# Two tiles transposed by DMA in place of TensorE, and two KV accumulations moved forward, in a linear-attention and SwiGLU kernel

## The chip, the core and the metric

The kernel runs on one core of a Trainium2 chip. A core has five engines, each with its own in-order instruction stream: TensorE (PE, matrix products; its weight loads are listed as PEld), VectorE (DVE), ScalarE (ACT), GpSimd (POOL) and SyncE (SP), which here issues nearly all DMAs. Engines wait for one another through semaphores. Operands live in SBUF (128 partitions); TensorE writes to PSUM, eight banks of 128x512 fp32.

The metric is the device time of one execution in microseconds, as a median of several executions. A smaller number is better.

## What is computed

The input x has 2048 rows (tokens) of 1024 values in bf16. Cut to what matters:

```python
xn = _layernorm(x)                                   # no affine part
q, k, v = split heads of (xn @ wqkv)                 # H = 32 heads of 32
phi = lambda t: where(t > 0, t + 1, exp(t)) + 1e-6
kv  = einsum("bhsd,bhse->bhde", phi(k), v);  z = sum over s of phi(k)
o   = (phi(q) @ kv) / (phi(q) . z + 1e-6)
s   = o @ wo
g   = silu((silu(xn @ w_gate) * (xn @ w_up)) @ w_down)   # F = 3584
return x + s * g
```

The KV matrix sums over all tokens, so all K and V products come before the first use of the attention's output.

## The kernel before

**Tiles.** x is cut into 16 tiles of 128 rows. For each tile, `x_load` brings it to SBUF, `ln_tile` normalises it and `t_tile` transposes it, so that the 1024 features lie on the partitions, as TensorE needs for a product over features. The transposed tiles of the first half of the tokens stay in the arena X, those of the second half in P.

**Normalising** (`ln_tile`, lines 767 to 795) is a chain of small operations: two statistics on VectorE (L772, L773), their aggregate (L778), an added epsilon (L779), a power on POOL (L782), and then, from tile two on, the negated mean on VectorE (L793) and the normalisation itself, one ScalarE activation of 128x1024 into W. The x tiles have four buffers, the normalised ones two: tile i uses buffer i mod 2, so tile four overwrites tile two's, and tile five tile three's.

**Transposing** (`t_tile`, lines 802 to 823) has two forms. Tiles below NPE (four before the change) are transposed by TensorE (L316): eight 128x128 transposes into one or more PSUM banks, and copies from there into X by ScalarE (L441) or VectorE (L823). Tiles two and three use one group of eight and one ScalarE copy of 128x1024 each. Tiles from NPE on are transposed by one DMA of SP (L808) from SBUF to SBUF, with no other engine.

**K and V products.** The first two tiles are multiplied plainly: eight calls of `p_piece`, each eight matmuls of 128x512. The other fourteen tiles go in seven pairs u = 1 to 7, and each pair has a K set (w = 0) and a V set (w = 1) (`kv_set`). A set multiplies two tiles by 1024 columns with seven products in place of eight (Winograd's form of Strassen's method). The products are numbered 1, 5, 2, 6, 7, 3, 4 in the order in which a set uses them; each is four matmuls of 128x512. Products 1, 2 and 4 take a transposed tile as it is: 1 and 2 the set's first tile, 4 its second. Products 5, 6, 7 and 3 take sums of the two tiles that VectorE makes (`x_sums`, four operations of 128x512 from X or P into W), so product 5 needs both tiles. The weights too need sums, made once on VectorE (`combos`).

A set's product 1 is copied to a second bank by ScalarE (`put1`), product 5 to SBUF (`put5`). VectorE adds product 5 in after products 6 and 7. A finished K block goes through `phi_evac` (an exponential on ScalarE, two operations on VectorE, L850 and L851), a V block through a ScalarE copy or, after product 7, a VectorE addition.

**KV accumulation.** `a_tile(i)` (lines 892 to 897) adds tile i's part to the KV matrix: eight matmuls of 128x129 into three banks that are kept for it. It needs all K and V blocks of tile i. The code puts these calls into a queue `fill` and takes one out in each set, after product 6 of the current set and product 1 of the next.

**What sets the order.** The code lists the operations in one program order, and `Plan` turns that into five instruction streams. It simulates the engines with costs written in the code. Each operation has a due time: the sum of TensorE's work listed ahead of its user, less the durations on the way. A DMA counts on that way as 4 us plus its bytes over 200 GB/s (line 112), and a transpose by DMA is entered with 400 KB, so it is due 6.05 us ahead of its user. VectorE, ScalarE, POOL and SP always take the ready operation that is due first. TensorE follows the program order, but may take an operation ahead of one that isn't ready, within a window of six (`WINDOW`). Then `tune` looks for gaps on TensorE and shifts due times where its simulation gets shorter. So any edit makes the whole order be planned again; on the chip the order of each engine is fixed.

The lines around the change, in the program order of the first tiles:

```python
ln_tile(2); p_piece(0, 1, 1); t_tile(2); combos(KVV[0], first[-1]); p_piece(1, 1, 1)
ln_tile(3); p_piece(0, 1, 0); t_tile(3); combos(KVV[1]);            p_piece(1, 1, 0)
```

After them come the first K set's products 1, 5 and 2 (L1001), and then the loop over the sets (L1003).

Of the kernel before, what the change touches and what calls it, by code (L numbers as in the profile page):

```python
# [316 lines left out]
    return last  # L317


def build_kernel(nc, A_x, A_wqkv, A_wo, B_w_gate, B_w_up, B_w_down, out, WINDOW=6, NWARM=15, NPE=4, LEAD=12.0):  # L320
    S, D, FF = 2048, 1024, 3584
    NT, KT, NG, NPAIR = 16, 8, 8, 14
    EPS_LN, EPS_PHI = 1e-5, 1e-6
# [9 lines left out]
    with ExitStack() as es:  # L333
# [20 lines left out]
        def named(*key):  # L354
            return Region([key])
# [50 lines left out]
        def bfree(b):  # L406
            freed[b] = len(PL.ops)
            (bare if b in is_bare else banks).append(b)
# [19 lines left out]
        def pe_mm(reads, writes, mms):  # L428
            return PL.op("pe", reads, writes, partial(_mm_group, mms), mm_cost(mms))
# [142 lines left out]
        for n in range(NWARM):  # L572
            b = n % 8
            m = 512 if n > 3 else 128
# [281 lines left out]
        def kv_ap(g):  # L856
            return ps[kvb[g // 3]][:, (g % 3) * 129:(g % 3) * 129 + 129]
# [34 lines left out]
        def a_tile(i):  # L892
            q = i % 4
            pk = pkv[i].ap()
            mms = [(kv_ap(g), pk[:, g * 128:(g + 1) * 128], vext[q][:, g, 0:129], i == 0 and g % 3 == 0, i == NT - 1)
                   for g in range(NG)]
            pe_mm([pkv[i].r, named("vx", q, 0), named("vx", q, 1), named("vx1", q), vx_r[q]], [bank_r[b] for b in kvb], mms)

        def x_sums(u):

            c = xs_ring.take()
            cv = c.ap(FP16).rearrange("p (m q t) -> p m q t", m=4, t=128)
            cr = [c.sub(q * KB, KB).r for q in range(4)]
            A = {(k, i): xt_half(2 * u + i, k) for k in range(2) for i in range(2)}
            ra = [xt_r(2 * u), xt_r(2 * u + 1)]
            tt(ra, [cr[0]], cv[:, 0], A[0, 1], A[1, 1], ALU.add, True)
            tt(ra + [cr[0]], [cr[1]], cv[:, 1], cv[:, 0], A[0, 0], ALU.subtract, True)
            tt(ra, [cr[2]], cv[:, 2], A[0, 0], A[0, 1], ALU.subtract, True)
            tt(ra + [cr[1]], [cr[3]], cv[:, 3], A[1, 0], cv[:, 1], ALU.subtract, True)

            def stat(m):
                if m in (1, 2, 4):
                    k, i = {1: (0, 0), 2: (1, 0), 4: (1, 1)}[m]
                    return [xt_ap(2 * u + i, 4 * k + q) for q in range(4)], ra[i]
                q4 = {5: 0, 6: 1, 7: 2, 3: 3}[m]
                return [cv[:, q4, q, :] for q in range(4)], cr[q4]
            return stat
# [56 lines left out]
        p_piece(1, 1, 0)  # L974
        for b in tb:
            bfree(b)
        fill = deque([partial(a_tile, 0), partial(a_tile, 1)])
        stats_of = {1: x_sums(1)}
        todo = [(u, w) for u in range(1, NT // 2) for w in range(2)]

        def prepare(u):
            if u >= NT // 2:
                return
            for i in (2 * u, 2 * u + 1):
                if i + 2 < NT:
                    x_load(i + 2)
            for i in (2 * u, 2 * u + 1):
                ln_tile(i)
                t_tile(i)
            stats_of[u] = x_sums(u)  # L990
# [3 lines left out]
        def kvs(n):  # L994
            if n not in sets and n < len(todo):
                u, w = todo[n]
                sets[n] = kv_set(u, w, stats_of[u])
            return sets.get(n)

        kvs(0)  # L1000
        for m in (1, 5, 2):  # L1001
            sets[0].step(m)
        for n in range(len(todo)):  # L1003
            cur = kvs(n)
            if todo[n][1] == 0:
                prepare(todo[n][0] + 1)
            nxt = kvs(n + 1)
            for m, k in ((6, 1), (7, 5), (3, 2), (4, 0)):
                cur.step(m)
                if nxt is not None and k:  # L1010
                    nxt.step(k)
                if k == 1 and fill:
                    fill.popleft()()
            if todo[n][1] == 1:
                while fill:
                    fill.popleft()()
                fill.extend((partial(a_tile, 2 * todo[n][0]), partial(a_tile, 2 * todo[n][0] + 1)))
# [730 lines left out]
def bass_recurrent_scan__linear_attn_block__swiglu_ffn__prompt_kernel(  # L1748
    nc: bass.Bass,
    A_x: bass.AP,  # L1750
    A_wqkv: bass.AP,
    A_wo: bass.AP,
    B_x: bass.AP,
    B_w_gate: bass.AP,
    B_w_up: bass.AP,
    B_w_down: bass.AP,
    out: bass.AP,
):
    build_kernel(nc, A_x, A_wqkv, A_wo, B_w_gate, B_w_up, B_w_down, out)
# [28 lines left out]
```

## Time and profile before

| | us |
|---|---|
| median of 5 runs | 716.21 (715.53 to 717.33) |
| profiled execution, its own time | 715.76 |
| span of its instructions | 714.0 |
| TensorE busy | 706.9 |
| VectorE busy | 641.7 |
| ScalarE busy | 404.5 |
| first transpose on TensorE (tile zero) starts | 6.54 |
| transposes of tiles two, three start | 18.11, 22.88 |
| first, second KV accumulation start | 24.19, 34.06 |
| first transpose by DMA (tile four) issued | 26.25 |

TensorE's granted clock is full in each slice of the span. All durations come from one profiled execution. In a timeline row the columns are start, length, engine and line, operation, what it writes and from what, how many instructions are merged in it, and in brackets the idle time of the engine before it and what ended that. Rows of one engine can overlap, because the matmuls are pipelined: the next starts before the one before has ended. The engine's name with a q is its instruction queue.

### The profile page before, as it was taken

To read this page: it belongs to the slowest core of one execution; us is meant where nothing else is said; L and a number is where in the kernel's file an instruction comes from. 1 tells how busy PE (TensorE), PEld (TensorE's weight loads), DVE (VectorE), ACT (ScalarE), POOL (GpSimd) and SP (SyncE) were. 2 spreads that over 40 slices of the span, in tenths; PEclk is the share of its full clock that TensorE was granted. 3 is DMA by queue.
4 is the path that set the end of the run, shared out by engine and by line. 5 is a ranking of instruction groups with operands and counts; after the bars stand their busy time and mean duration, and the time that the engine had idled before them with its cause. 6 is when DMAs were issued, how large, how long until landed. Compare 5 with 4: busy or idle time off the path is not lost.

```text
span 714.0 us, 11277 instructions
## 1 busy us (share of the span) xinstructions
PE 706.9 (99%) x4149; PEld 390.7 (55%) x4149; DVE 641.7 (90%) x1533; ACT 404.5 (57%) x779; POOL 12.5 (2%) x35
## 2 busy tenths in 40 slices
PE   8999999999999999999999999999999999999997
PEld 4444445555555555556556455555555555565654
DVE  7999988989999999998957999999999999798863
ACT  3666654887679675664122157676886656621212
POOL 2011000000000000000000000000000000000000
PEclk9999999999999999999999999999999999999999
DMA  9425335146364344225595964132715241656653
GB/s 306 107 60 118 60 117 177 60 125 215 135 186 130 126 137 134 86 84 164 149 197 164 257 169 148 60 118 92 202 66 177 89 148 60 175 143 161 143 155 95
DMA packets 138759, 98.11 MB, mean 137 GB/s; under 512 B 32849, under 2 KB 135761, under 8 KB 138705
## 3 DMA queue, kind: packets, MB, share of 16 engines
q1 hardware_dynamic: 138416, 97.21, 48.3%
q8 instruction: 32, 0.52, 0.3%
q10 hardware_dynamic: 288, 0.20, 0.1%
q14 instruction: 23, 0.18, 0.1%
HBM read 77.59 MB, written 12.71 MB: 126 GB/s over the span
## 4 chain that ended last, share of the span: by engine, by line
PE 91%; DVE 4%; DMA 2%; ACT 1%; issue 0%; SPq 0%; DVEq 0%
PE ps L309 91%; DMA X<-in_A_wqkv_dram 1%; DMA H<-in_A_wqkv_dram 1%; DVE TM L452 1%; DVE W L452 1%; DVE ps L452 1%; DVE X L452 1%; DVE H L851 1%; ACT TM L441 0%; ACT W L441 0%; DVE H L1035 0%; DVE P L452 0%; SPq L455 0%; ACT ps L441 0%; ACT L441 0%
## 5 line engine op out<-in xcount | busy, mean ns | idle before, releaser
L309 PE MATMUL ps<-X,W 128*128 128x512 f16 (+2 forms) x1372 | 289.2, 350 | 0.1
L441 ACT ACTIVATE TM<-ps 128x512 f16<-128x512 f32 (+3 forms) x355 | 186.7, 547 | 106.6 <-PE ps L309 102.8
L309 PE MATMUL ps<-H,W 128*128 128x512 f16 (+2 forms) x1096 | 218.9, 351 | 0.1
L452 DVE TENSOR_TENSOR W<-W 128x1024 f16<-128x1024 bf16 (+5 forms) x416 | 187.4, 487 | 6.2 <-PE ps L309 5.4
L309 PEld LDWEIGHTS ps<-X,W 128*128 128x128 f16 (+1 forms) x1372 | 132.7, 98 | 103.8 <-DVE ps L452 0.8
L309 PEld LDWEIGHTS ps<-H,W 128*128 128x128 f16 (+1 forms) x1096 | 106.2, 98 | 95.0 <-DVE ps L452 0.6
L452 DVE TENSOR_TENSOR ps<-ps,TM 128x256 f32<-128x256 f32 (+1 forms) x250 | 132.5, 532 | 12.6 <-PE ps L309 10.2
L441 ACT ACTIVATE ps<-ps 128x512 f32<-128x512 f32 (+1 forms) x174 | 85.4, 491 | 100.9 <-PE ps L309 100.5
L309 PE MATMUL ps<-P,W 128*128 128x256 f16 (+1 forms) x516 | 99.8, 319 | 0.4 <-DVE W L452 0.4
L441 ACT ACTIVATE H<-ps 128x512 f16<-128x512 f32 (+1 forms) x126 | 74.8, 604 | 41.4 <-PE ps L309 41.4
L452 DVE TENSOR_TENSOR H<-H 128x1024 f16<-128x1024 f16 (+5 forms) x126 | 71.9, 587 | 0.6 <-ACT H L441 0.4
L309 PEld LDWEIGHTS ps<-P,W 128*128 128x128 f16 (+1 forms) x516 | 50.3, 98 | 29.7 <-DVE W L452 0.7
L441 ACT ACTIVATE TM<-TM 128x512 f16<-128x512 f32 (+1 forms) x61 | 38.1, 626 | 48.8 <-DVE TM L452 48.8
L309 PE MATMUL ps<-W 128*128 128x256 f16 (+1 forms) x330 | 61.8, 282 | 0.2 <-DVE ps L452 0.2
L452 DVE TENSOR_TENSOR TM<-ps,TM 128x512 f32<-128x512 f32 (+3 forms) x63 | 41.8, 664 | 12.8 <-PE ps L309 12.1
L452 DVE TENSOR_TENSOR H<-H,TM 128x512 f16<-128x512 f16 x112 | 45.5, 420 | 8.4 <-ACT H L441 8.1
L309 PEld LDWEIGHTS ps<-W 128*128 128x128 f16 (+1 forms) x330 | 31.7, 98 | 32.2 <-DVE ps L452 2.3
L309 PE MATMUL ps<-H,X 128*128 128x512 bf16 (+1 forms) x150 | 35.6, 379 | 0.9 <-ACT ps L441 0.6
L309 PE MATMUL ps<-H,P 128*128 128x512 bf16 (+1 forms) x110 | 26.8, 379 | 0.0
L452 DVE TENSOR_TENSOR H<-ps,TM 128x512 f16<-128x512 f32 (+1 forms) x35 | 24.2, 690 | 2.6 <-PE ps L309 2.1
L452 DVE TENSOR_TENSOR TM<-TM,W 128x512 f16<-128x512 f16 (+1 forms) x39 | 14.4, 370 | 10.5 <-ACT TM L441 10.5
L309 PEld LDWEIGHTS ps<-H,X 128*128 128x128 f16 (+1 forms) x150 | 14.0, 98 | 17.1 <-ACT ps L441 1.1
(97 smaller groups left out, 433.8 us busy)
## 6 DMA issues: line engine op xcount, KB each, us to landing
W<-in_B_w_gate_dram SPq DMA_DIRECT2D x14, 1024.0 KB, 5.2
W<-in_B_w_up_dram SPq DMA_DIRECT2D x13, 1024.0 KB, 5.5
W<-in_B_w_down_dram SPq DMA_DIRECT2D x14, 896.0 KB, 6.1
H<-in_A_wqkv_dram SPq DMA_DIRECT2D x8, 512.0 KB, 8.0
H<-r_scratch SPq DMA_DIRECT2D x32, 128.0 KB, 3.5
W<-m_scratch SPq DMA_DIRECT2D x4, 1024.0 KB, 5.3
s_scratch<-TM SPq DMA_DIRECT2D x32, 128.0 KB, 2.3
TM<-in_A_x_dram SPq DMA_DIRECT2D x16, 256.0 KB, 3.4
```

The source lines that it names most:

```text
L309: last = h.matmul(o, l, r, start=st, stop=sp, skip_group_check=True)
L441: q = PL.op("act", reads, writes, lambda h: h.activation(o, i, func, **kw), nel(o) / (1000.0 if "bias" in kw or not isinstance(kw.get("sca ...
L452: return dve(reads, writes, lambda h: h.tensor_tensor(o, a, b, op), nel(o), 1.92 if fast else 0.96)
L851: dve([src_r, b.r], [out_r], lambda h: h.scalar_tensor_tensor(out_ap, src, 0.0, ba, ALU.max, ALU.add), 512)
```

## The change

The default of NPE goes from 4 to 2, so tiles two and three of x take the DMA form of `t_tile`. The queue `fill` starts empty; `a_tile(0)` is listed after product 1 of the first K set, and `a_tile(1)` after product 5, ahead of product 2. Later accumulations keep their places in the program order.

```diff
-def build_kernel(nc, A_x, A_wqkv, A_wo, B_w_gate, B_w_up, B_w_down, out, WINDOW=6, NWARM=15, NPE=4, LEAD=12.0):
+def build_kernel(nc, A_x, A_wqkv, A_wo, B_w_gate, B_w_up, B_w_down, out, WINDOW=6, NWARM=15, NPE=2, LEAD=12.0):
...
-        fill = deque([partial(a_tile, 0), partial(a_tile, 1)])
+        fill = deque()
...
         for m in (1, 5, 2):
             sets[0].step(m)
+            if m != 2:
+                a_tile(m // 5)
         for n in range(len(todo)):
```

## The prediction

> **What bounds the kernel now.** I read the page first, then the waits of TensorE, then the time around the change engine by engine: TensorE's timeline, the chain of work, VectorE's windows, the transposes by DMA. From the page:
>
> ```profile
> span 714.0 us, 11277 instructions
> PE 706.9 (99%) x4149; PEld 390.7 (55%) x4149; DVE 641.7 (90%) x1533; ACT 404.5 (57%) x779; POOL 12.5 (2%) x35
> ```
>
> TensorE (PE) is busy 706.9 of 714.0 us. So only two things shorten the run: work taken off TensorE, and idle time closed. All its named waits are few:
>
> ```profile
> PE ps L309 <- DVE TM L570: 1.0, 1, 1.0
> PE ps L316 <- DVE W L789: 0.8, 1, 0.8
> PE ps L309 <- ACT ps L441: 0.6, 1, 0.6
> PE ps L316 <- DVE TM L452: 0.6, 1, 0.6
> ```
>
> The first two lie before the first tile is transposed, the fourth at the end; the change touches only the third, 0.6 us. The timeline of TensorE shows where it lies:
>
> ```profile
> 18.11 0.61 PE L316 MATMUL ps<-ident,W 128*128 128x128 f16 x8
> 18.56 4.48 PE L309 MATMUL ps<-H,X 128*128 128x512 bf16 x20
> 22.88 0.61 PE L316 MATMUL ps<-ident,W 128*128 128x128 f16 x8
> 23.32 1.03 PE L309 MATMUL ps<-H,X 128*128 128x512 bf16 x4
> 24.19 0.63 PE L309 MATMUL ps<-H,TM 128*128 128x129 bf16 x8
> ...
> 28.87 1.04 PE L309 MATMUL ps<-H,X 128*128 128x512 bf16 x4 [0.59 <-ACT ps L441]
> ```
>
> The two rows on ident are the transposes of tiles two and three. 23.32 is product 1 of the first K set (tiles two and three), 24.19 the first KV accumulation (tile zero), 28.87 product 2 of the V set, which waits 0.59 us for ScalarE. The chain of work shows how ScalarE came to be late:
>
> ```profile
> 23.08 0.47 ACT H L441
> 23.55 0.03 issue
> 23.57 1.02 ACT X L441
> 24.59 0.49 ACT ps L441
> 25.08 2.27 ACT W L441 x2
> 27.35 0.97 ACT TM L441 x2
> 28.32 0.50 ACT ps L441
> 28.82 0.05 issue
> 28.87 21.21 PE ps L309 x115
> ```
>
> ScalarE runs without a break from 23.57 to 28.82, and the first step of that run is the 1.02 us copy of tile three out of PSUM.
>
> **The transposes on TensorE go.** Two groups of eight: the next row starts 18.56 - 18.11 = 0.45 and 23.32 - 22.88 = 0.44 us later. These starts, and not the 0.61 us durations, are the price, since matmuls are pipelined. Sum: **-0.89 us**, on the path, as TensorE has work on both sides. The Trainium skill (VectorE: DVE Perf Modes, "The three transpose paths") gives 390 ns for a 128x128 transpose on TensorE; by it sixteen would cost 6.2 us and the change would gain that much. The trace's pace is 56 ns, and I take the trace.
>
> **Their copies go too**, two of 1.02 us on ScalarE. The first (18.76) has nothing behind it that is late. The second heads the unbroken run above. Without it the last step ends at about 28.82 - 1.02 = 27.80. TensorE, which now runs dry at 28.28 (28.87 - 0.59), would get there at 28.28 - 0.89 + 0.47 = 27.86, the 0.47 being the second accumulation, which moves ahead of this place. So the wait closes: **between -0.59 and 0**. I take -0.5, since the products also change places among themselves and some of the wait may come back.
>
> **The accumulations move.** Each takes 24.66 - 24.19 = 0.47 us at the start-to-start pace; moving costs nothing by itself. What they read is there: the last K evacuation of tile one (L851) ends at 19.84, the V evacuations at 22.92 and 23.68, against earliest places of about 23.3 and 23.8. The second used to stand at 34.06, where VectorE is full; as filler it is missed there, which I count below.
>
> **What the DMA adds.** Two transposes on SP's queue:
>
> ```profile
> L808 SPq DMA_TRANSPOSE X<-W x4: 1237/1280/1342, 26.2 to 46.8; - x4
> DMA to landing us min/median/max: 3.0/3.1/3.5
> L1592 SPq DMA_TRANSPOSE TM<-TM x30: 1190/1214/3775, 355.3 to 705.1; - x30
> DMA to landing us min/median/max: 2.4/2.6/7.6
> ```
>
> Each holds SP's queue 1.24 us and lands a whole 128x1024 tile in 3.0 to 3.5 us here, up to 7.6 us later on, among the weight loads. The Trainium skill speaks against the change: its same table puts DMA at 1309 ns for a 128x128 block. Eight blocks in a row would be an estimated 10.5 us; tile three, ready at 22.43, would land at 32.9 and leave TensorE idle for some 7 us. Twelve rows at L808 of the same shape say 3.0 to 3.5 us, so I use these for the likeliest and the 7.6 for the range.
>
> *Tile two* leaves normalisation at 17.86 (ScalarE, 16.62 + 1.24). Its transpose is issued about 17.9, when the initial weight load still drains, and an x load issued at 17.88 took 4.7 us to land. So it lands between 20.9 and 22.6. Its first user, product 1 of the K set, moves to 23.32 - 0.89 = 22.43, and the accumulation of tile zero can fill a gap. Cost 0 to 0.2; I take 0.
>
> *Tile three* leaves normalisation at 22.43 if nothing is reordered, and lands at 25.5 to 26.0; the first operand sum on VectorE takes 0.42 us, so product 5 could start at 25.9 to 26.4. The cover: from 22.43 on TensorE has product 1 (0.86), both accumulations (0.94), product 2 (0.86) and product 1 of the V set (0.86), all of which do without tile three, and that the planner's window of six lets ahead: 3.52 us, to 25.95. Stall 0 to 0.45. But the planner counts a transpose by DMA as 6 us ahead of its user, so tile three's normalisation gets a due time some 4 us earlier. In the trace its x tile landed at 15.4, its statistics start at 17.10, and its small operations on VectorE and POOL end at 21.16 for work of about 2.8 us: 1.3 us can come out of that stretch alone, which brings the landing to about 24.3. I take a stall of 0. Without the two accumulations between, the cover is 2.58 us and the same landing at 25.5 would stall product 5 by about 0.9.
>
> *Who waits behind them.* SP issues in order: x tiles six and seven (17.88, 22.45) go out 1.2 us later, and tiles four and five's transposes (26.25) follow. Tile six's statistics are taken after 36.0, so 10 us of slack. Normalised tiles four and five reuse two and three's buffers and now wait for the DMA's read to land: 22.6 against 24.99, and 24.3 to 25.5 against 26.2. Cost 0; with tile three at 27 or later ScalarE would be held, and the next set with it. POOL does one power (0.55 us) per tile and idles otherwise.
>
> **What VectorE gives back.** Its windows:
>
> ```profile
> 18.00:28.00 10.00, 10.00 (x66) 5.16 (x64) 9.36 (x27) 8.50 (x12) 1.64 (x3) 1.00 0.31 90
> 28.00:40.00 12.00, 11.40 (x60) 5.34 (x59) 11.85 (x26) 5.99 (x11) 0.12 (x1) 1.00 0.34 80
> ```
>
> Columns: window, length, then busy PE, PE weight loads, VectorE, ScalarE, POOL. From 18 to 40 us VectorE is busy 21.2 of 22, and its work isn't reduced. TensorE 1.4 us early meets a VectorE that can be at most 0.8 us early. So up to 0.6 us may return as short waits between 28 and 45; after 50 VectorE has 4 us spare in 50 (45.90 busy). I take +0.2: LayerNorm of later tiles and operand sums can be put off.
>
> **Sum:** -0.89 - 0.5 + 0 + 0.2 = **-1.2 us**: span 714.0 to 712.8, the profiled execution 715.76 to 714.6. That execution is 0.45 us under the median of 716.21, so the median goes to **715.0** (-0.17%). A measurement of this kernel tells about 0.2% (1.43 us) from no change, so this sits just inside.
>
> **The rivals.**
> *VectorE takes it all back.* For it: 97% busy in 28 to 40. Against it: 0.8 us of idle time that it can use. The gain shrinks to 0.2 to -0.5 us of loss: 716.0 to 716.7.
> *More than the sum.* A replanned order also closes a little of the idle time later (TensorE's named waits from 50 us on sum to 1.2 us, half of it at the very end) and all 0.59 goes: -1.5 to -2.1 us, 714.1 to 714.7. For it: the order is recomputed whole. Against: nothing later is aimed at.
> *Slower: tile three lands late at product 5.* Place: 25.95 on TensorE. Each microsecond of landing after 25.5 costs one. Landing 4.7 us after issue (as the x load) at 22.45 stalls TensorE by 1.6 us and gives about 716.6; the 7.6 us row gives a landing at 30.0, a stall of 4.5 and 719.5. It decides (slower by 0.2%) from a landing at about 28.2, 5.7 us after the issue. Against: DMA share falls to near nothing after 20 us.
> *The work isn't moved at all:* excluded, sixteen transposes leave the program.
>
> **How the numbers follow.** Chances: forecast (714.3 to 715.8) 0.48; more than the sum 0.16; VectorE takes it back 0.18; late tile three or a worse replanned order 0.18. Faster by over 0.2% means under 714.78: the second case and 0.42 of the first, 0.36. Slower means over 717.64: the last case where it is beyond its point, 0.16. The rest is 0.48. The range reaches from 713.8 (leaving 0.05 below) to 717.8 (leaving 0.14 above); the likeliest case's own is 714.3 to 715.8.
>
> **What the changed profile would show.** L316 of TensorE with sixteen instructions fewer; the 128x1024 copies into X at L441 gone; L808 into X with six issues. TensorE's timeline after the last piece: product 1, two 128x129 groups within 3 us, then product 5 without a wait on VectorE's sums; no 0.59 us wait for ScalarE near 28. Wrong would be a wait of product 5 on the W sum (late tile three), short waits on VectorE between 28 and 45 that sum to over 0.6, or new idle time past 100 us, where no step of mine reaches.

## The result, and the profile after

The changed kernel takes 714.9 us (713.81 to 715.82) against 716.3 us (714.96 to 717.64) for the kernel before, measured anew beside it. The ratio is 0.9981, with a 95% interval of 0.9975 to 0.9987. So it is faster, by 1.4 us, which is 0.19%: clear of no change by its interval, and just inside the 0.2% that the prediction had set as its bound. Two later measurements of the same kernel gave 0.9984 (0.9975 to 0.9992) and 0.9985 (0.9976 to 0.9993), that is 1.1 to 1.2 us.

The page of the changed kernel, first lines:

```profile
span 713.2 us, 11248 instructions
PE 706.2 (99%) x4133; PEld 389.7 (55%) x4133; DVE 641.0 (90%) x1533; ACT 403.4 (57%) x777; POOL 13.2 (2%) x35
```

Sixteen matmuls and two ScalarE instructions are gone, VectorE has as many as before. The waits of TensorE:

```profile
PE ps L309 <- DVE TM L570: 1.0, 1, 1.0
PE ps L316 <- DVE W L789: 0.7, 1, 0.7
PE ps L309 <- DVE ps L452: 0.6, 1, 0.6
PE ps L316 <- DVE TM L452: 0.6, 1, 0.6
PE ps L309 <- DVE W L452: 0.4, 1, 0.4
```

The 0.6 us wait for ScalarE has left the list. A wait for VectorE's PSUM work has come (0.6 us, third row); it lies near 409 us, far from the change, and the last section shows that it differs between executions of the same order. TensorE's timeline around the change:

```profile
11.14 12.27 PE L309 MATMUL ps<-H,X 128*128 128x512 bf16 x56
23.25 1.10 PE L309 MATMUL ps<-H,TM 128*128 128x129 bf16 x16
24.19 1.89 PE L309 MATMUL ps<-H,X 128*128 128x512 bf16 x8
26.02 2.85 PE L309 MATMUL ps<-H,W 128*128 128x512 f16 x12
28.70 1.03 PE L309 MATMUL ps<-H,X 128*128 128x512 bf16 x4
29.56 2.75 PE L309 MATMUL ps<-H,W 128*128 128x512 f16 x12
32.15 1.03 PE L309 MATMUL ps<-H,X 128*128 128x512 f16 x4
33.17 1.90 PE L309 MATMUL ps<-H,W 128*128 128x512 f16 x8
```

No transposes stand in it. After the plain products and product 1 of the first K set (within the 56) come both accumulations (23.25, sixteen matmuls), then product 2 and the V set's product 1 (24.19), then product 5 (26.02). That is the order which the prediction gave. Idle time can be read from the starts: 512-wide matmuls start 0.216 us apart, so eight from 24.19 end their turn at 25.92, and the next starts at 26.02, 0.10 later. From 26.02 twelve lead to 28.61 against 28.70, 0.09; from 32.15 four lead to 33.01 against 33.17, 0.16. Together 0.35 us between 23 and 40 us. In the kernel before, the four from 27.25 led to 28.11 and the next started at 28.87: 0.76 us, which the profile named as 0.59. The sum for the stretch is then -0.89 for the transposes and -0.41 for idle time: -1.30 us. In the two later profiles of the changed kernel the idle time of the stretch is 0.23 and 0.27 us.

The two tiles' own DMAs, and VectorE's windows:

```profile
L808 SPq DMA_TRANSPOSE X<-W x6: 1237/1289/1522, 16.3 to 44.4; - x6
DMA to landing us min/median/max: 3.0/3.0/4.4
18.00:28.00 10.00, 10.00 (x59) 4.78 (x57) 9.86 (x26) 7.25 (x11) 2.59 (x3) 1.00 0.77 162
28.00:40.00 12.00, 12.00 (x56) 5.23 (x55) 11.74 (x26) 6.38 (x11) 0.55 (x1) 1.00 0.22 62
```

Tile two's transpose was issued at 16.26 and landed 4.4 us later, at 20.7, while the first weights still came in. Tile three's was issued at 20.89 and landed at 23.9. VectorE is busy 9.86 of 10 us from 18 to 28 (9.36 before): it used the idle time that it had.

### The profile page after: what moved, and what is told of

Its sections match the earlier page's. It is cut to its first block, busy times and chain, and to the rows that moved or that the text cites. A ratio compares the mean times of both kernels' runs of the same rounds, so it can differ in the third digit from the quotient of the medians.

```text
span 713.2 us, 11248 instructions
## 1 busy us (share of the span) xinstructions
PE 706.2 (99%) x4133; PEld 389.7 (55%) x4133; DVE 641.0 (90%) x1533; ACT 403.4 (57%) x777; POOL 13.2 (2%) x35
## 4 chain that ended last, share of the span: by engine, by line
PE 92%; DVE 4%; DMA 2%; ACT 1%; issue 0%; SPq 0%; DVEq 0%
PE ps L309 92%; DMA X<-in_A_wqkv_dram 1%; DMA H<-in_A_wqkv_dram 1%; DVE TM L452 1%; DVE W L452 1%; DVE ps L452 1%; DVE H L851 1%; DVE X L452 0%; ACT TM L441 0%; DVE H L1037 0%; DVE P L452 0%; SPq L455 0%; ACT L441 0%; DVE TM L850 0%; PE ps L316 0%
## 5 line engine op out<-in xcount | busy, mean ns | idle before, releaser
L309 PE MATMUL ps<-X,W 128*128 128x512 f16 (+2 forms) x1372 | 289.2, 350 | 0.1
L309 PE MATMUL ps<-H,W 128*128 128x512 f16 (+2 forms) x1096 | 218.5, 351 | 0.1
L309 PEld LDWEIGHTS ps<-X,W 128*128 128x128 f16 (+1 forms) x1372 | 132.7, 98 | 103.7 <-DVE ps L452 0.8
L309 PEld LDWEIGHTS ps<-H,W 128*128 128x128 f16 (+1 forms) x1096 | 105.9, 98 | 95.6 <-DVE ps L452 1.1
L309 PE MATMUL ps<-P,W 128*128 128x256 f16 (+1 forms) x516 | 99.8, 319 | 0.4 <-DVE W L452 0.4
L309 PEld LDWEIGHTS ps<-P,W 128*128 128x128 f16 (+1 forms) x516 | 50.3, 98 | 29.7 <-DVE W L452 0.7
L309 PE MATMUL ps<-W 128*128 128x256 f16 (+1 forms) x330 | 61.8, 282 | 0.7 <-DVE ps L452 0.6
L309 PEld LDWEIGHTS ps<-W 128*128 128x128 f16 (+1 forms) x330 | 31.7, 98 | 32.7 <-DVE ps L452 2.8
L309 PE MATMUL ps<-H,X 128*128 128x512 bf16 (+1 forms) x150 | 35.4, 379 | 0.3 <-DMA H<-in_A_wqkv_dram 0.2
L309 PE MATMUL ps<-H,P 128*128 128x512 bf16 (+1 forms) x110 | 26.8, 379 | 0.0
L309 PEld LDWEIGHTS ps<-H,X 128*128 128x128 f16 (+1 forms) x150 | 14.2, 98 | 17.3 <-DMA H<-in_A_wqkv_dram 0.9
```

Source lines behind the costliest of these rows:

```text
L309: last = h.matmul(o, l, r, start=st, stop=sp, skip_group_check=True)
```

## The experiments

The theory after the result: 0.9 us come from the transposes and the rest from the ScalarE wait, which the 1.02 us copy had caused. Rivals: the newly planned order brings the gain whatever was edited; or the accumulations do. A single profile's span is not used for differences below 1 us here, for a reason told at the end; times are medians, and idle time is read from starts inside a stretch.

**Parts put back with the order kept.** Three kernels keep every engine's planned order of the changed kernel and only insert instructions whose results nothing uses. A fourth is the changed kernel as it is. Of the first one's edit, the lines that insert:

```diff
...
+        eight = [("x", lambda h, k=k: h.transpose(pbs[:, k, :], ident[:, :], ident[:, :])) for k in range(8)]
+        for m in ("piece", "first"):         # in mid-pieces; ahead of the K set's product 1
+            put_before("pe", mark[m].fn, *eight)
+        put_before("act", mark["put1"].fn, ("x", lambda h: h.activation(   # ahead of put1
+            P.at(0, 2 * KB, FP16), H.at(KV0[1], 2 * KB), ACT.Identity)))
...
```

With both insertions:

> The changed kernel in its own planned order, with sixteen unused 128x128 transposes put back into TensorE's stream (eight in the middle of the K and V pieces, eight ahead of product 1 of the first K set) and one unused 128x1024 copy into ScalarE's, ahead of the first product's copy. Theory (the gain is 0.9 us of transposes and the ScalarE wait): 1.0 to 1.5 us slower than the changed kernel, so within 0.4 us of the kernel before, with a TensorE wait for ScalarE back near 29 us. Rival (the gain comes from the newly planned order): within 0.3 us of the changed kernel, some 1.3 us faster than before.

With the transposes alone:

> The changed kernel in its own planned order, with only the sixteen unused transposes put back into TensorE's stream. Theory: 0.6 to 0.9 us slower than the changed kernel (0.9 of work, of which up to 0.3 may fall into the short waits at products 5), so 0.5 to 0.8 us faster than before. Rival (transposes lie beside something else, the order makes the gain): no more than 0.2 us slower than the changed kernel.

With the copy alone:

> The changed kernel in its own planned order, with only an unused 128x1024 copy of about 1 us put into ScalarE's stream ahead of the first product's copy. Theory (that copy heads the run of ScalarE work that made TensorE wait 0.6 us): a wait of TensorE for ScalarE of 0.1 to 0.6 us near 29 us, total 0.1 to 0.6 us slower than the changed kernel. Rival (ScalarE has room, the wait went because the order changed): no new wait, total the same within 0.2 us.

The changed kernel beside them:

> The changed kernel as it is, beside the three others. All theories: 1.2 to 1.5 us faster than before. If the longer wait near 409 us of its profile (0.8 against 0.3 us) belongs to the order, it is there again at 0.8; if it is chance of one execution, it differs from 0.8.

| kernel | median us | ratio to before (95%) |
|---|---|---|
| before, beside these four | 716.34 | 1 |
| changed kernel | 715.23 | 0.9984 (0.9975 to 0.9992) |
| transposes back | 715.72 | 0.9992 (0.9983 to 1.0001) |
| copy back | 715.22 | 0.9984 (0.9976 to 0.9993) |
| both back | 715.98 | 0.9992 (0.9983 to 1.0001) |

The transposes cost 0.5 us by the medians, a little under the 0.6 to 0.9 expected; with 0.6 us of uncertainty to each side that doesn't settle their size. Both parts cost 0.75 us, under the 1.0 to 1.5 of the theory and over the 0.3 of its rival. What the transposes take on TensorE can be read from the trace. TensorE's timeline of the kernel with both parts back shows their price and what became of the copy (the inserted lines move L309 to L311 in these kernels):

```profile
20.03 0.61 PE L1742 MATMUL ps<-ident 128*128 128x128 f16 x8
20.48 4.48 PE L311 MATMUL ps<-H,X 128*128 128x512 bf16 x20
24.80 0.61 PE L1742 MATMUL ps<-ident 128*128 128x128 f16 x8
25.24 1.03 PE L311 MATMUL ps<-H,X 128*128 128x512 bf16 x4
26.11 1.10 PE L311 MATMUL ps<-H,TM 128*128 128x129 bf16 x16
27.08 1.90 PE L311 MATMUL ps<-H,X 128*128 128x512 bf16 x8
28.82 2.75 PE L311 MATMUL ps<-H,W 128*128 128x512 f16 x12
31.41 0.81 PE L311 MATMUL ps<-H,X 128*128 128x512 bf16 x3
```

Each group takes 0.45 and 0.44 us, start to start, as in the kernel before. But no wait is left: 27.08 leads to 28.81 against 28.82, and 28.82 to 31.41, where the V set's product 2 starts. All the work of the kernel before is there, and its 0.76 us of idle time is not. The copy alone did make a wait, at another place than expected:

```profile
23.88 1.10 PE L311 MATMUL ps<-H,TM 128*128 128x129 bf16 x16
25.30 1.90 PE L311 MATMUL ps<-H,X 128*128 128x512 bf16 x8 [0.32 <-ACT ps L443]
```

Product 2 waits at 25.30 for the copy of product 1, which stands right behind the inserted one. It waits 0.48 us by the starts (23.88 and 0.94 are 24.82). With the transposes back as well, eight of them stand between the last plain piece and product 1, so TensorE comes 0.44 us later, and 0.03 us of the wait are left (26.11 and 0.94 are 27.05, against 27.08). In the time the copy alone cannot be seen (715.22 against 715.23). So the theory is half right: the transposes are on the path, but the copy brings no wait back at the V set's product 2, where the old one was.

**One part alone, the order planned anew.**

```diff
-def build_kernel(nc, A_x, A_wqkv, A_wo, B_w_gate, B_w_up, B_w_down, out, WINDOW=6, NWARM=15, NPE=4, LEAD=12.0):
+def build_kernel(nc, A_x, A_wqkv, A_wo, B_w_gate, B_w_up, B_w_down, out, WINDOW=6, NWARM=15, NPE=2, LEAD=12.0):
```

> Tiles two and three transposed by DMA, the accumulations left in their old places; the order is planned anew. Theory (the two accumulations are the cover for tile three's landing): product 5 waits 0.5 to 1.2 us, so 0.4 to 0.9 us faster than before and 0.5 to 0.9 slower than the full change. Rival (no cover is needed, as tile three lands near 24 us): as fast as the full change, 1.2 to 1.5 us faster than before.

This is the kernel before with the transposes alone. For the accumulations alone, the changed kernel with NPE=4:

> The accumulations moved forward, tiles two and three still transposed by TensorE; the order is planned anew. Theory (moving costs and brings nothing by itself; the 1.02 us copy still keeps ScalarE late): 0 to 0.4 us faster than before, a wait for ScalarE of 0.3 to 0.6 us near 29 us. Rival (the accumulations as filler are the gain): 0.8 us faster or more.

The transposes by DMA alone took 715.40 us against 716.89 us: 0.9981 (0.9973 to 0.9988), the rival's number. The accumulations alone took 716.33 us: 0.9995 (0.9986 to 1.0003), and kept the wait for ScalarE. This newly planned order is thus no gain by itself. TensorE's timeline, and below it the chain of work that led to the wait:

```profile
28.83 1.03 PE L309 MATMUL ps<-H,W 128*128 128x512 f16 x4
30.39 0.81 PE L309 MATMUL ps<-H,X 128*128 128x512 bf16 x3 [0.54 <-ACT ps L441]
```

```profile
24.60 4.40 PE ps L309 x32
29.00 0.02 issue
29.03 0.60 ACT TM L441
29.62 0.50 ACT ps L441
```

The row at 30.39 lists three of four matmuls; with the missing one ahead of it, the wait from start to start was about 0.5 us and not 0.7. The 1.02 us copy is in this kernel, yet it isn't in the chain: ScalarE had caught up and waited for TensorE to finish the K set's product 2 (29.00). Then came the exponential of its K block (29.03), and only then the V set's copy of product 1 (29.62), for which TensorE waited. In the kernel before, the same exponential started at 27.73, and product 2 had ended at 27.41 (26.38 and 1.03). By an estimate from these, ScalarE without the copy could have been 0.3 us earlier there at the most, so the copy made less than half of the wait of the kernel before (0.76 us by the starts).

So the moved accumulations are not what makes it faster. As that was against my expectation, the transposes alone were measured again beside the full change, together with the kernels of the last group below.

> The transposes by DMA alone, beside the full change on the same chip. Theory, as it stands after the first look (the planner brings the first accumulation forward by itself, so the listed place brings next to nothing): the same as the full change within 0.3 us. Rival (the first look was luck): 0.5 us or more slower than the full change.

> The changed kernel beside the three others: 1.2 to 1.5 us faster than before by every theory; idle TensorE time from 23 to 40 us 0.2 to 0.35 us.

They took 715.50 us (0.9989, 0.9980 to 0.9998) and 715.72 us (0.9985, 0.9976 to 0.9993): the same. TensorE's timeline of this second measurement of the transposes alone:

```profile
25.68 0.63 PE L309 MATMUL ps<-H,TM 128*128 128x129 bf16 x8
26.61 2.76 PE L309 MATMUL ps<-H,W 128*128 128x512 f16 x12 [0.30 <-DVE W L452]
```

The planner brought the first accumulation ahead of product 5 by itself, within its window of six, though it is listed behind product 6. Product 5 waits 0.46 us by the starts (0.34 in the first measurement), against 0.10 or less in the full change. It doesn't wait for the landing: tile three had landed at 24.6, and VectorE took the first operand sum at 26.14, behind sums of weights. The second accumulation as cover is worth some 0.3 us on TensorE, and the full change's 0.16 us near 33 us, which this kernel does not have, takes half of that back.

**What had caused the wait.** In the kernel before, TensorE had done product 5 of the K set (25.52) ahead of product 2 (26.38), and had only four matmuls on sums (27.25) between that and the V set's product 2 (28.87):

```profile
25.52 1.03 PE L309 MATMUL ps<-H,W 128*128 128x512 f16 x4
26.38 1.03 PE L309 MATMUL ps<-H,X 128*128 128x512 bf16 x4
27.25 1.03 PE L309 MATMUL ps<-H,W 128*128 128x512 f16 x4
```

In the changed kernel tile three comes late, so product 2 goes first. This kernel leaves everything as before and only lists the products in the new order:

```diff
-        for m in (1, 5, 2):
+        for m in (1, 2, 5):
             sets[0].step(m)
```

> The kernel before, transposes on TensorE and accumulations where they were, but the first K set's products listed as 1, 2, 5 in place of 1, 5, 2. Theory (the ScalarE wait of the kernel before came from its order: product 2 late, so its K block and its bank late, so the V set's product 5 behind product 2): the wait of 0.6 us for ScalarE near 28.9 goes, idle TensorE time from 23 to 40 us falls from 0.76 to under 0.4, total 0.3 to 0.7 us faster than before. Rival (only the 1.02 us copy made that wait): the wait stays at 0.4 to 0.7 us and the total is within 0.2 us of before.

With the transposes by DMA on top:

> The transposes by DMA and the products listed as 1, 2, 5, accumulations where they were. Theory: no wait for ScalarE, product 5 waits under 0.4 us; as fast as the full change (1.2 to 1.5 us faster than before), at best 0.2 us better. Rival (moving the accumulations matters): 0.4 us or more slower than the full change.

The timeline of the first, with the transposes on TensorE:

```profile
23.90 0.61 PE L316 MATMUL ps<-ident,W 128*128 128x128 f16 x8
24.35 1.03 PE L309 MATMUL ps<-H,X 128*128 128x512 bf16 x4
25.21 0.63 PE L309 MATMUL ps<-H,TM 128*128 128x129 bf16 x8
25.68 1.89 PE L309 MATMUL ps<-H,X 128*128 128x512 bf16 x8
27.41 4.66 PE L309 MATMUL ps<-H,W 128*128 128x512 f16 x20
31.90 1.89 PE L309 MATMUL ps<-H,X 128*128 128x512 bf16 x8
```

and of its ScalarE:

```profile
24.59 1.02 ACT L441 ACTIVATE X<-ps 128x1024 f16<-128x1024 f16 x1
```

The transposes and the 1.02 us copy are there, and the wait is gone: 27.41 leads to 31.73 against 31.90, 0.17 us in place of 0.76. Twenty matmuls on sums run in a row, where the kernel before had only four before it needed ScalarE. TensorE is 1.0 us later here than in the kernel before (24.35 against 23.32), but that isn't the cause: with the accumulations alone it was as late (24.44), and in the old order it waited. The time, 716.36 us against 716.53 with a ratio of 0.9993 (0.9984 to 1.0002), allows the expected 0.3 to 0.7 us and no change alike; the idle time tells them apart. That the new order by itself removes the wait, with the copy in place, is shown. Why the planner has more products ready then (the bank of product 2 is free earlier for the V set's product 5) is only argued from the order.

The changed kernel's own trace agrees. Its ScalarE:

```profile
22.59 0.60 ACT L441 ACTIVATE H<-ps 128x512 bf16<-128x512 f32 x1 [0.27 <-PE ps L309]
27.72 0.58 ACT L441 ACTIVATE ps<-ps 128x512 f32<-128x512 f32 x1
```

The first row is the evacuation of the last plain piece (23.08 in the kernel before), the second the V set's copy. The copy ends at 28.30, 5.7 us after the first row; in the kernel before it ended at 28.82, also 5.7 us after. So ScalarE is no sooner there without its 1.02 us copy. What moved is the place where TensorE needs it: 28.61 less 22.59 are 6.0 us, against 5.0 (28.11 less 23.08), because the second accumulation and a third product on sums stand ahead of it.

The combination brought nothing: 716.20 us, 0.9992 (0.9983 to 1.0001). In its profile product 5 waits 0.93 us for VectorE's sum, where under 0.4 was expected: tile three had landed at 24.1, but VectorE took its first operand sum at 26.18. No version beats the changed kernel beyond what can be measured.

**The slower rival: tile three late.** The changed kernel in its own order, with unused 1 MB loads on SP's queue ahead of tile three's transpose:

```diff
+        put_before("sp", mark["tx", 3].fn, *[("i", lambda h, n=n: h.dma_start(
+            P.at(n * 8 * KB, 8 * KB).rearrange("p (kt c) -> p kt c", c=512),
+            wqkv_v[:, :, n * 512:n * 512 + 512]), late, 16) for n in range(1)])      # or range(2)
...
```

> The changed kernel in its own planned order, with one unused load of 1 MB on SP's queue ahead of tile three's transpose, which lands about 3 us later (27 in place of 23.9). Theory (from a landing at about 25.5 each microsecond costs TensorE one): product 5 starts near 27.5 in place of 26.0, total 1.0 to 1.8 us slower than the changed kernel, so about as fast as before. Rival (there is other work that TensorE can do, or it is caught up later): under 0.5 us slower than the changed kernel.

> The same with two unused loads of 1 MB: tile three lands about 6 us later, near 30. Theory: product 5 starts near 30.5, total 4.0 to 5.0 us slower than the changed kernel, 2.6 to 3.6 slower than before. Rival (caught up later): under 2 us slower than the changed kernel.

With one load tile three landed at 27.4, and TensorE's timeline has

```profile
24.94 1.89 PE L311 MATMUL ps<-H,X 128*128 128x512 bf16 x8
27.86 2.84 PE L311 MATMUL ps<-H,W 128*128 128x512 f16 x12 [1.04 <-DVE W L454]
```

Product 5 starts 0.5 us after the landing and 1.19 us after its turn (24.94 and eight starts are 26.67). The time is 716.73 us against 716.89: ratio 1.0 (0.9992 to 1.0008), so some 1.1 us lost against the changed kernel's 0.9984, as much as the wait: no sign that it is caught up later. With two loads it landed at 31.6, and the time is 722.23 us: 1.0077 (1.0065 to 1.0090), 5.3 us slower than before and 6.6 slower than the changed kernel, beyond the 4 to 5 expected. Its timeline and windows tell why:

```profile
25.34 1.89 PE L311 MATMUL ps<-H,X 128*128 128x512 bf16 x8
32.11 5.30 PE L311 MATMUL ps<-H,W 128*128 128x512 f16 x12 [4.88 <-DVE W L454]
37.20 1.10 PE L311 MATMUL ps<-H,X 128*128 128x512 bf16 x4
```

```profile
22.00:27.00 5.00, 4.95 (x35) 2.69 (x34) 4.70 (x14) 3.53 (x6) 1.85 (x2) 1.00 1.09 347
27.00:32.00 5.00, 0.23 (x2) 0.00 (x0) 0.37 (x2) 0.32 (x2) 0.00 (x0) 0.85 1.25 199
32.00:37.00 5.00, 4.89 (x12) 1.79 (x13) 3.65 (x9) 2.11 (x3) 0.00 (x0) 0.50 0.77 183
37.00:42.00 5.00, 4.95 (x22) 2.10 (x22) 4.09 (x10) 2.45 (x5) 0.00 (x0) 0.97 0.00 0
```

The columns are as in the prediction, and behind POOL's stands the granted clock: 1.00, 0.85, 0.50, 0.97. TensorE stood for 5.0 us (25.34 and eight starts are 27.07), and then ran its twelve matmuls at half speed, 0.424 us apart in place of 0.216: another 2.5 us. The two make 7.5 us in this profile; the 6.6 of the medians, with 0.9 us of uncertainty from the five runs of this kernel alone, allows that. A mean of 0.85 over 27 to 32 us is half speed in the last 1.5 of them, so from about 30.5, some 3.4 us after TensorE had stopped. The one-load kernel, with 1.2 us of idle time, kept a clock of 1.00. The Trainium skill ("TensorE: Matmul & The Clock Gate", Part 1) says that the clock drops to half after an idle window of about 3.4 us; the two runs lie on either side of that figure and agree with it.

## Why the prediction was right, and where its steps were not

The time was forecast as 715.0 us and came as 714.9, in the range and on the expected side; the gain was forecast as 1.2 us and came as 1.4, and as 1.1 to 1.2 in the later measurements. For one of its two main terms the reason was not the one given, so that the sum came out as well as it did was in part luck. By steps:

- *Transposes, -0.89.* Right in the trace: they are gone, and put back they take 0.45 and 0.44 us again. By the medians they cost 0.5 us, which 0.6 us of uncertainty lets agree. The trace's pace of 56 ns held, not the table's 390 ns.
- *The ScalarE wait, -0.5.* It went whole: 0.76 us by the starts, of which 0.35 came back as the short waits below. The net of -0.41 us stands against -0.3 in the forecast (-0.5 and +0.2). The reason failed. "Their copies go too" said that the wait closes because the 1.02 us copy no longer heads ScalarE's run. But the kernel with the products listed as 1, 2, 5 keeps the copy and loses the wait; the kernel with both parts put back has no wait either; and in the changed kernel the V set's copy ends as long after the last plain piece as before (5.7 us). What closed it is the order: product 2 stands ahead of product 5, and three products on sums in place of one lie between it and the V set's product 2. I had read the chain of work, which names what was late, as if the piece at its head were what set its end. The step also left out that the exponential in the chain needs product 2, which ended at 27.41: without the copy alone, by the estimate above, 0.3 us would have gone. No run took out the copy with the old order kept.
- *Tile three, stall 0.* Landing was forecast at about 24.3 and measured at 23.9. Product 5 started 2.1 us after it all the same, since VectorE's order has sums of weights (23.67, 24.94) ahead of the operand sum (25.54). That the order was planned for a later landing is likely, as the planner counts 6 us for it, but not shown. The price was 0.10 us.
- *Cover.* "Without the two accumulations between, the cover is 2.58 us" failed: the planner's window lets the first accumulation through by itself, so the cover is 3.05 us. The wait was 0.34 to 0.46 us instead of 0.9, set by VectorE's order and not by the landing, and the total the same as with the accumulations moved.
- *Give-back of VectorE, +0.2.* Found as 0.16 us near 33 us and 0.09 us before it, both ended by a VectorE instruction. The prediction's sign of being wrong, new idle time past 100 us, came in the first profile (near 409 us) and not in the second; the last section has it.
- *The slower rival.* Its mechanism held, and its slope of one to one for the first 1.2 us. Its bound of 25.5 for the landing moves with TensorE: in the run with one load TensorE came 0.75 us later (24.94 against 24.19), so that the landing at 27.4 was 1.2 us beyond the bound and not 1.9. What it lacked is the clock: with two loads the price was 6.6 us by the medians, where the profile has 2.5 us from matmuls at half speed.

## What to carry to other kernels

A wait at the end of a busy chain of another engine can be closed by changing what TensorE does first, as well as by shortening that chain; before crediting a removed instruction, put it back with the order kept. On a TensorE that is busy 99% of the time, small transposes are worth moving to DMA when the products that don't need them cover the landing, but the cover has to keep TensorE's idle time short, as a long stall (5.0 us here; 1.2 us was not yet one) is paid twice, once as idle time and once at half clock.

## What the runs showed that was not expected

The first weights reach TensorE at times that differ between executions of the same instructions by some 2 us. In the profiles of the kernel before and of the changed kernel the wait for them is 0.2 us; in that of the kernel with both parts back, whose first instructions are the same as the changed kernel's, it is 2.0 us:

```profile
PE ps L311 <- DMA H<-in_A_wqkv_dram: 2.0, 3, 1.1
```

A second place is near 409 us, where TensorE waited for VectorE 0.6 us in the first profile of the changed kernel, 1.0 us in the third and not at all in the second, with the same order each time. This wait can also take up a delay from before it: the second profile was 1.3 us behind the first at 404 us (405.54 against 404.24 for the same matmul) and 0.5 behind at 410 us (410.51 against 410.03). What makes it vary stays open. That is why the span of a single profile told less here than the idle time within a stretch: the first profile's span is only 0.8 us shorter than that of the kernel before, while the medians differ by 1.4 us.
